# A fused attention and MLP kernel: key sums of batch 0 in a PSUM bank of their own, one load moved, more filler products, and a new order of the whole program

## The chip, the cores and the metric

The kernel runs on one core of a Trainium2 chip. The metric is the time of one execution on the device in microseconds (us). A core has five engines that run side by side, each with its own in-order instruction stream: TensorE (PE in the profile; its weight loads are listed as PEld), VectorE (DVE), ScalarE (ACT), GpSimd (POOL) and SyncE (SP), which here only issues DMA transfers. They meet through semaphores: an instruction that waits holds up everything behind it on its own engine.

## What is computed

The first half is linear attention with a quadratic feature map. With a = x S1^T and b = x S2^T (8 numbers each), the features of a row are the 64 products of a and b. For each of 4 batches and 4 heads, over 1088 rows of 32 numbers:

```python
def phi(x):
    a = np.einsum('rd,bhsd->bhsr', S1, x)
    b = np.einsum('rd,bhsd->bhsr', S2, x)
    return np.einsum('bhsi,bhsj->bhsij', a, b).reshape(*x.shape[:-1], r * r)
q_p, k_p = (phi(q), phi(k))
kv = np.einsum('bhsf,bhsd->bhfd', k_p, v)
z = np.sum(k_p, axis=2)
num = np.einsum('bhsf,bhfd->bhsd', q_p, kv)
den = np.einsum('bhsf,bhf->bhs', q_p, z)[..., None] + 1e-06
return num / den
```

The second half takes the result as 4352 tokens of 128 numbers (x) and applies an MLP with a leaky activation, h = x w_in (128 to 2048), g = max(h, 0) + alpha min(h, 0), out = g w_out. The kernel uses g = (1 - alpha) max(h, 0) + alpha h, so that the MLP is relu(h) times the weights w_a = (1 - alpha) w_out, plus x times one 128x128 matrix W = w_in (alpha w_out).

## The kernel before

Nothing is written in program order. The code makes a list of operations, each with the engines that may run it, an estimated duration, the operations that it depends on, and the buffers that it holds. A list scheduler, `plan()` (L174), walks this list with estimated times, picks an engine and a buffer slot for each operation, and returns the order in which they are emitted. An operation's place is steered by its due time, which is worked out backwards from its users and then moved by a constant from the table `SHIFT` (L65 to L171). The arrival times of the first loads are constants too, in `FIRST` (L371). So a change of constants alone moves hundreds of instructions, and with a place moves the engine and the PSUM bank. On the chip only the emitted order and the semaphores count.

The names of operations, which the text below uses:

- `k0.0T`, `k0.0Tc`, `k0.0ab`, `k0.0abc`, `k0.0kp0` and `kp1`: the keys of batch 0, first half of the row blocks. They are transposed on TensorE (L625), copied to SBUF, multiplied by S1 and S2 (L635), copied to the tile ab (L360 or L362, one helper line for all copies), and multiplied out into the features kp (L652). `k0.1...` is the second half, `kr0.0...` the 64 rows left over. Batches 1 to 3 are transposed on VectorE (L679) and do both halves in one product.
- `kv0.0`, `kv0.1`, `kvr0`: features times v, summed in one PSUM bank (L698, L712), and the sums of the key features, which come from a times b (L704, L715). In the kernel before, both kinds sit in one bank, and the sums are the last products of each of these operations.
- `zm0`, `finz0`, `zc0`: the key sums are spread out (VectorE, L728), multiplied (TensorE, L734), and reduced to the tile zc (VectorE, L740 and L741). `kvc0`, `fin0`, `kvW0` do the same for the sums with v: a copy, a transpose (L743), a copy to the tile kvW.
- `q0.0T`, `q0.0a`, `q0.0b`, `q0.0ac0`, `q0.0ac1`, `q0.0mul0`, `q0.0mul1`: the first 512 queries of batch 0 are transposed (VectorE, L832), multiplied by S1 and S2 in two rounds (TensorE, L849), and multiplied out (a copy, L360 or L362, and a product on VectorE, L861).
- `q0.0den`, `q0.0num` (TensorE, L762), `q0.0dT`, `q0.0rc`, `q0.0rr` (VectorE, L769 to L778: transpose, reciprocal, transpose back), `q0.0x0` (VectorE, L784): the quotient, which is the MLP's input xT. `q0.1...` is the second 512 of batch 0; q1, q2, q3 and qr are the other batches and the left-over rows, with L792, L805 and L819 in place of L832, L849 and L861.
- `h0.0` to `h0.15` (TensorE, L931): 16 products of 128x512 for 512 tokens, four PSUM banks at most in flight; `r0.0` to `r0.15`: relu to bf16 (ScalarE L937, or VectorE L939); `o0.0` to `o0.15` and `W0` (TensorE, L952, or L949 in the last group): products summed in PSUM bank 7. The first number is the group: 0 to 6 have 512 tokens each, 7 to 9 have 256. `oT` and `st` transpose and store.
- `w_in_bf` (cast of w_in, L360), `w_a`, `w_b`, `w_hi`, `w_lo` (made of w_out, L555, L564, L572, and a cast), `winT` (L588), `Wmm` (L597), `W`: the weights are prepared inside the kernel, each in four or two parts, in between the rest.

All loads but three small ones are issued on SP's queue in the order of the code (L445 to L468). The first are k0.0, k0.1, kr0.0, v0.0, q0.0, v0.1, vr0.0, q0.1, w_in0, w_out0, w_in1, w_out1.

Before `h0.0` there is also filler: `dummy()` (L496) multiplies ones into bank 7, whose content is not used. Seven stand at the start (`warm`, L500); `plan()` counts further ones from its own estimate of TensorE's idle time ahead of an operation (L256), and L1013 emits them in front of it:

```python
o.fill = max(0, int((t - free_at["pe"] - 350) / DUMMY)) if 4000 < t < FILL else 0
```

## Time and profile before

| | us |
|---|---|
| median of 5 executions (lowest, highest) | 114.19 (113.84, 115.08) |
| the profiled execution, its own time | 113.85 |
| its span, first to last instruction | 112.1 |
| so outside the span | 1.75 |
| first MLP product `h0.0` starts | 17.30 |
| last product ends, by the chain | 108.84 |

The profile page gives each engine's busy time. The timeline lists runs of like instructions with start and duration; a product's duration there includes its way through the array, so that the distance from one start to the next tells how fast they follow each other. The list of waits says for which engine an idle one waited, and the chain of work that ended last follows, from the last instruction back, what released each step.

### The profile page before, as it was taken

What the parts mean: (1) busy time and instruction counts of PE and PEld (TensorE: products, weight loads), DVE (VectorE), ACT (ScalarE), POOL (GpSimd) and SP (SyncE); (2) the same over time, 40 slices, a digit from 0 to 9 for tenths busy, and PEclk for the clock granted to TensorE, in tenths of its full rate; (3) what the DMA queues carried; (4) which work ended last, traced back from release to release, by engine and by line L of the source; (5) the groups of instructions that cost most, each with busy time, mean ns of one, the idle gap of its engine ahead of it and who ended that gap; (6) DMA issues with size and microseconds to landing.
All of it is one profiled execution on the core that took longest, in us unless ns stands there. A gap on an engine that the chain in (4) does not pass through costs nothing.

```text
span 112.1 us, 3537 instructions
## 1 busy us (share of the span) xinstructions
PE 104.6 (93%) x1455; PEld 54.2 (48%) x1455; DVE 83.3 (74%) x157; ACT 75.5 (67%) x163; POOL 25.3 (23%) x25
## 2 busy tenths in 40 slices
PE   7997777999999999999999999999999999999980
PEld 2664442463664352344466254444334344588970
DVE  3176689896899878989854397748698798788750
ACT  2542589999709863479947474987596197678860
POOL 3060089779800006480000600000000000000000
PEclk9999999999999999999999999999999999999999
DMA  2899899869849961005002200032050022023131
GB/s 77 242 304 280 241 281 314 179 122 340 149 56 327 231 99 29 0 6 94 0 6 47 46 6 0 0 53 46 0 94 0 6 47 47 3 47 61 33 58 47
DMA packets 37536, 11.25 MB, mean 100 GB/s; under 512 B 27008, under 2 KB 37520, under 8 KB 37520
## 3 DMA queue, kind: packets, MB, share of 16 engines
q1 hardware_dynamic: 37264, 10.95, 41.7%
q8 instruction: 11, 0.18, 0.8%
q10 hardware_dynamic: 256, 0.08, 0.3%
q14 instruction: 5, 0.04, 0.1%
HBM read 8.80 MB, written 2.23 MB: 98 GB/s over the span
## 4 chain that ended last, share of the span: by engine, by line
PE 85%; DVE 7%; ACT 3%; issue 1%; POOL 1%; DVEq 0%
PE ps L952 27%; PE ps L931 26%; PE ps L762 8%; PE ps L805 5%; PE ps L635 4%; PE ps L498 3%; PE ps L698 2%; PE ps L849 2%; PE ps L949 2%; PE ps L625 1%; PE ps L734 1%; DVE qT__75 L792 1%; DVE aq__77 L819 1%; DVE aq__76 L861 1%; DVE kT__64 L679 1%
## 5 line engine op out<-in xcount | busy, mean ns | idle before, releaser
L931 PE MATMUL ps<-xT__96,w_in_bf 128*128 128x512 bf16 (+1 forms) x80 | 22.0, 357 | 1.7 <-DVE xT__96 L784 1.3
L931 PEld LDWEIGHTS <-w_in_bf 128*128 128x128 bf16 x160 | 15.2, 97 | 16.7 <-issue 5.0
L952 PEld LDWEIGHTS <-w_a_bf 128*128 128x128 bf16 x144 | 13.5, 98 | 14.3 <-issue 3.2
L931 PE MATMUL ps<-xT__97,w_in_bf 128*128 128x512 bf16 (+1 forms) x80 | 18.5, 337 | 0.0
L937 ACT ACTIVATE rh__82<-ps 128x512 bf16<-128x512 f32 (+1 forms) x21 | 11.5, 548 | 5.6 <-PE ps L931 5.3
L937 ACT ACTIVATE rh__83<-ps 128x512 bf16<-128x512 f32 (+1 forms) x18 | 9.8, 545 | 4.9 <-PE ps L931 4.5
L652 POOL TENSOR_TENSOR kp__70<-ab__67 128x1024 f32<-128x1024 f32 (+1 forms) x3 | 5.0, 1658 | 28.0 <-ACT ab__67 L360 28.0
L937 ACT ACTIVATE rh__85<-ps 128x512 bf16<-128x512 f32 (+1 forms) x19 | 10.8, 566 | 0.5 <-PE ps L931 0.5
L937 ACT ACTIVATE rh__86<-ps 128x512 bf16<-128x512 f32 (+1 forms) x16 | 8.9, 557 | 2.2 <-PE ps L952 1.9
L360 ACT COPY aq__76<-ps 128x1024 f32<-128x1024 f32 (+1 forms) x7 | 5.6, 833 | 5.6 <-PE ps L805 3.5
L937 ACT ACTIVATE rh__84<-ps 128x512 bf16<-128x512 f32 (+1 forms) x15 | 7.8, 519 | 1.0 <-PE ps L931 0.9
L769 DVE STREAM_TRANSPOSE dt__78<-ps 128x1024 f32<-128x1024 f32 (+2 forms) x6 | 5.6, 932 | 3.6 <-PE ps L762 3.6
L952 PE MATMUL ps<-rh__82,w_a_bf 128*128 128x512 bf16 (+1 forms) x22 | 7.8, 354 | 0.0
L952 PE MATMUL ps<-rh__84,w_a_bf 128*128 128x512 bf16 (+1 forms) x21 | 7.6, 360 | 0.0
L952 PE MATMUL ps<-rh__83,w_a_bf 128*128 128x512 bf16 (+1 forms) x20 | 7.3, 364 | 0.0
L937 ACT ACTIVATE rh__87<-ps 128x512 bf16<-128x512 f32 (+1 forms) x12 | 6.8, 569 | 0.6 <-PE ps L931 0.5
L952 PE MATMUL ps<-rh__85,w_a_bf 128*128 128x512 bf16 (+1 forms) x20 | 7.1, 353 | 0.0
L952 PE MATMUL ps<-rh__86,w_a_bf 128*128 128x512 bf16 (+1 forms) x19 | 6.8, 358 | 0.0
L959 DVE STREAM_TRANSPOSE oT__91<-ps 128x512 f32<-128x512 f32 (+1 forms) x8 | 5.4, 681 | 1.3 <-PE ps L952 1.1
L939 DVE TENSOR_SCALAR rh__84<-ps 128x512 bf16<-128x512 f32 x8 | 5.5, 682 | 1.2 <-PE ps L952 1.1
L778 DVE STREAM_TRANSPOSE rr__80<-dt__78 128x1024 f32<-128x1024 f32 (+2 forms) x6 | 5.6, 932 | 0.2
L952 PE MATMUL ps<-rh__87,w_a_bf 128*128 128x512 bf16 (+1 forms) x16 | 5.7, 354 | 0.0
(165 smaller groups left out, 213.8 us busy)
## 6 DMA issues: line engine op xcount, KB each, us to landing
out_dram<-oT__91 SPq DMA_DIRECT2D x28, 64.0 KB, 1.9
k<-in_k_dram SPq DMA_DIRECT2D x3, 512.0 KB, 5.6
q<-in_q_dram SPq DMA_DIRECT2D x3, 512.0 KB
v<-in_v_dram SPq DMA_DIRECT2D x12, 128.0 KB, 6.0
w_in_f<-in_moe_w_in_dram SPq DMA_DIRECT2D x2, 512.0 KB, 8.2
w_out_f<-in_moe_w_out_dram SPq DMA_DIRECT2D x2, 512.0 KB, 6.5
k<-in_k_dram SPq DMA_DIRECT2D x2, 256.0 KB, 2.8
v<-in_v_dram SPq DMA_DIRECT2D x2, 256.0 KB, 3.7
```

Of the source, the lines that this page charges most:

```text
L360: nc.scalar.copy(dst, src)
L635: nc.tensor.matmul(ps(bf)[lo + i:lo + i + aw, j * 64:(j + 1) * 64], sb(bT)[:, j * cnt + i:j * cnt + i + aw], S12blk.rearrange("p h c -> p ...
L652: (nc.vector if e == "dve" else nc.gpsimd).tensor_tensor(out=dst, in0=i0, in1=i1, op=ALU.mult)
L762: nc.tensor.matmul(dst, w, mv, start=True, stop=True, skip_group_check=True)
L769: nc.vector.transpose(bview(sb(dt), [[1, nn]]).rearrange("p (c n) -> p c n", c=2), ps(bd)[:, :, :ncp])
L778: o = op("dve", dv(nn) + 35, lambda e: nc.vector.transpose(sb(rr)[:, :nn], bview(sb(dt)[:, :, 1], [[32, nb], [0, 32]])), [o], [dt, rr], 80 ...
L805: nc.tensor.matmul(ps(bufs[t // 2])[64 * c:64 * c + 64, t % 2, :nf], bview(Sab[32 * t:32 * t + 32, i], [[1, R]]), moving(sb(bq), t, c), st ...
L931: nc.tensor.matmul(ps(b)[:, :n], w_in_bf[:, c * 128:(c + 1) * 128], xs(), start=True, stop=True)
L937: nc.scalar.activation(sb(br)[:, :n], ps(b)[:, :n], ACTF.Relu)
L939: nc.vector.tensor_scalar_max(sb(br)[:, :n], ps(b)[:, :n], 0.0)
L952: nc.tensor.matmul(ps(bo)[:, :n], w, y(), start=c == 0, stop=c == NC)
L959: o = op("dve", dv(n) + 40, lambda e: nc.vector.transpose(bview(sb(boT), [[1, n]]), ps(bo)[:, :n]), [last], [bo, boT], 80, end, f"oT{g}")
```

## The change

There are four parts.

1. For batch 0 the key sums get operations of their own, `z0.0`, `z0.1` and `zr0`, in a bank of their own (`bzs`), which depend on ab alone. `kv0.0`, `kv0.1` and `kvr0` keep the products with v, and `zm0` reads the new bank as soon as `zr0` is done. For batches 1 to 3 the same products stand where they stood.
2. The load of q0.0 is issued one place earlier, before v0.0 rather than after it.
3. Filler is counted with 150 ns rather than 350 ns taken off the planned gap, up to `h0.0` instead of up to a planned 12.5 us.
4. `SHIFT`, `FIRST` and the planned rate of v's later loads have new values, so that the order, the engine and the bank of operations are new in the whole program.

The two programs' opening, in the order in which each engine gets it (a number in brackets: that many fillers ahead; loads left out):

```
TensorE before: warm k0.0T rowsT k0.1T k0.0ab kr0.0T alphaT k0.1ab [2]kv0.0 q0.0a q0.0b kr0.0ab kv0.1
  [1]kvr0 [1]finz0 fin0 q0.0den q0.0num winT0 q0.1a q0.1b h0.0 h0.1 h0.2 h0.3 h0.4 h0.5 h0.6 o0.0 h0.7
  o0.1 o0.2 h0.8 o0.3 k1.0ab q0.1den h0.9 k1.1ab
TensorE after:  warm k0.0T rowsT k0.1T k0.0ab alphaT k0.1ab z0.0 kr0.0T [1]z0.1 kr0.0ab q0.0a q0.0b zr0
  [2]finz0 kv0.0 kv0.1 kvr0 q0.0den fin0 [3]q0.0num [1]q0.1a q0.1b h0.0 h0.1 h0.2 h0.3 h0.4 q0.1den h0.5
  h0.6 h0.7 o0.0 h0.8 o0.1 h0.9 o0.2 o0.3 winT1 h0.10 o0.4 k1.0ab h0.11 h0.12 o0.5 winT0
VectorE before: ... k0.0kp1 q0.0T k0.1kp0 alpha q0.0ac1 q0.0mul0 kr0.0kp q0.0mul1 zm0 q0.1T zc0 q0.0dT q0.0rc
  q0.0rr q0.0x0 q0.1mul0 q0.1mul1 r0.3 k1.0T k1.1T
VectorE after:  ... alpha k0.0kp0 q0.0T k0.1kp0 kr0.0kp q0.0ac1 zm0 q0.0mul1 q0.0mul0 zc0 q0.1T q0.0dT q0.0rc
  q0.0rr w_hi0 q0.0x0 q0.1mul1 q0.1mul0 r0.1 r0.3 q0.1dT r0.4 k1.0T k1.1T
ScalarE before: ... q0.0ac0 kr0.0abc kvc0 w_in_bf kvW0 w_in_bf w_a1 w_hi0 q0.1ac1 q0.1ac0 w_in_bf w_in_bf
  r0.0 r0.2 r0.1 r0.6 r0.7 r0.4 r0.5
ScalarE after:  ... kr0.0Tc kr0.0abc q0.0ac0 kvc0 w_in_bf w_in_bf kvW0 w_b1 w_hi1 q0.1ac1 q0.1ac0 w_in_bf
  w_in_bf r0.2 r0.0 w_b3 r0.7 r0.5 r0.8 r0.6
GpSimd before:  ident identb k0.0kp0 k0.1kp1 w_b0 w_a0 w_lo0 w_b3 w_a2 w_a3 w_b2 w_lo2 k1.1kp k1.0kp
GpSimd after:   ident k0.0kp1 k0.1kp1 identb w_b0 w_a1 w_a0 w_b2 w_lo0 w_lo1 w_a3 w_a2 w_lo3 k1.1kp k1.0kp
```

From `h0.0` on, TensorE's stream of bf16 products is interrupted by the fp32 products of the attention 16 times before and 20 times after. The diff, without the values of `SHIFT`:

```diff
-FILL, DUMMY = 12500, 220.0
+FILL, DUMMY = 20000, 220.0
 AHEAD = {"pe": 120, "act": 150, "dve": 250, "pool": 300, "sp": 0}
...
 SHIFT = {
...
 }
...
     holds = {b.stream: 0 for o in ops for b in o.bufs}
-    mode, count, there = 0, BEFORE, {0: 0.0, 1: 0.0}
+    mode, count, there, begun = 0, BEFORE, {0: 0.0, 1: 0.0}, False
     for o in reversed(ops):
...
         if e == "pe":
-            o.fill = max(0, int((t - free_at["pe"] - 350) / DUMMY)) if 4000 < t < FILL else 0
+            begun = begun or o.name == "h0.0"
+            o.fill = max(0, int((t - free_at["pe"] - 150) / DUMMY)) if 4000 < t < FILL and not begun else 0
             block, count = count // BLOCK, count + 2 * o.fill + o.ni
...
     state = {"t": 0.0}
-    FIRST = {"rows": 3900.0, "arows": 5000.0, "k0.0": 3800.0, "k0.1": 4700.0, "kr0.0": 5250.0, "v0.0": 6350.0,
-             "q0.0": 7350.0, "v0.1": 8300.0, "vr0.0": 8600.0, "q0.1": 9900.0, "w_in0": 11700.0, "w_out0": 13400.0,
-             "w_in1": 15200.0, "w_out1": 17000.0, "k1": 18600.0, "q1": 20400.0}
+    FIRST = {"rows": 4050.0, "arows": 4900.0, "k0.0": 3800.0, "k0.1": 4700.0, "kr0.0": 5900.0, "q0.0": 7100.0,
+             "v0.0": 8150.0, "v0.1": 9000.0, "vr0.0": 9200.0, "q0.1": 9850.0, "w_in0": 11600.0, "w_out0": 13000.0,
+             "w_in1": 15500.0, "w_out1": 17200.0, "k1": 19200.0, "q1": 20900.0}
     loads = {}
...
                  bass.AP(tensor=v.tensor, offset=(b * H * S + 256 * t) * D, ap=[[2 * D, 128], [S * D, H], [1, 2 * D]]),
-                 128 * H * 2 * D * 4, 115.0)
+                 128 * H * 2 * D * 4, 170.0)
 
...
     load_rest("k", k_rs[0], k, 0, (0,), "kr0.0")
+    load_q0(0)
     load_half("v", v_sb, v, 0, 0)
-    load_q0(0)
     load_half("v", v_sb, v, 0, 1)
...
 
-    rest_k = {}
+    rest_k, rest_ab = {}, {}
 
...
         for b in (2 * m, 2 * m + 1) if i is None else (2 * m + i,):
+            rest_ab[b] = o[0].deps[0]
             rest_k[b] = o + got(tag.replace("k", "v", 1))
...
                       lambda bkp=bkp: bview(sb(bkp), [[1, 1024]]), [bab], [bkp], kp_eng[hp], f"k{b}.{hp}", None if pe else turn)
-            halves.append((o, bab, bkp))
+            halves.append((o, bab, bkp, o[0].deps[0]))
         m, i = divmod(b, 2)
         bk = pk()
+        bzs = pk() if pe else bk
+        z0 = 0 if pe else R
+        rest = slice(i * SR, (i + 1) * SR)
+
+        def where(x, h):
+
+            return (x, h) if pe else (h // 2, 2 * x + h % 2)
 
...
             def f(e):
-                ab = [bview(sb(x[1]), [[1, 256]]) for x in halves]
                 kp = [bview(sb(x[2]), [[1, 1024]]) for x in halves]
...
                         for h in range(H):
-                            half, blk = (x, h) if pe else (h // 2, 2 * x + h % 2)
+                            half, blk = where(x, h)
                             nc.tensor.matmul(ps(bk)[32 * h:32 * h + 32, :R], v_sb[b][:, h, 4 * x + t if pe else 2 * t + x],
...
                                              start=x == t == 0, stop=False, skip_group_check=True)
+                if not pe:
+                    zs(xs)(e)
+            return f
+
+        def zs(xs):
+            def f(e):
+                ab = [bview(sb(x[1]), [[1, 256]]) for x in halves]
                 for x in xs:
                     for h in range(H):
-                        half, blk = (x, h) if pe else (h // 2, 2 * x + h % 2)
-                        nc.tensor.matmul(ps(bk)[32 * h:32 * h + 32, R:R + 32], ab[half][:, 32 * blk:32 * blk + 32],
+                        half, blk = where(x, h)
+                        nc.tensor.matmul(ps(bzs)[32 * h:32 * h + 32, z0:z0 + 32], ab[half][:, 32 * blk:32 * blk + 32],
                                          ab[half][:, 128 + 32 * blk:128 + 32 * blk + 32],
-                                         start=False, stop=False, skip_group_check=True)
+                                         start=pe and x == 0, stop=False, skip_group_check=True)
             return f
...
         def kvr(e):
-            s = slice(i * SR, (i + 1) * SR)
             for h in range(H):
-                nc.tensor.matmul(ps(bk)[32 * h:32 * h + 32, :R], v_rs[m][s, h], kp_rest[m][s, h],
+                nc.tensor.matmul(ps(bk)[32 * h:32 * h + 32, :R], v_rs[m][rest, h], kp_rest[m][rest, h],
                                  start=False, stop=True, skip_group_check=True)
+            if not pe:
+                zr(e)
+
+        def zr(e):
             for h in range(H):
-                nc.tensor.matmul(ps(bk)[32 * h:32 * h + r, R:R + r], ab_rest[m][s, 0, h], ab_rest[m][s, 1, h],
+                nc.tensor.matmul(ps(bzs)[32 * h:32 * h + r, z0:z0 + r], ab_rest[m][rest, 0, h], ab_rest[m][rest, 1, h],
                                  start=False, stop=True, skip_group_check=True)
+        oz = None
+        if pe:
+            for x in range(2):
+                oz = op("pe", 150, zs((x,)), [oz, halves[x][3]], [bzs, halves[x][1]], 200, name=f"z{b}.{x}", mode=1, ni=16)
+            oz = op("pe", 140, zr, [oz, rest_ab[b]], [bzs], 200, name=f"zr{b}", mode=1, ni=16)
         o = None
...
             hs = [halves[x] for x in xs] if pe else halves
-            bufs = [bk] + [x for h in hs for x in h[1:]]
-            o = op("pe", 600 * len(xs) + 30, kv(xs), [o] + [x for h in hs for x in h[0]] + (got(f"v{b}.{xs[0]}") if pe else got(f"v{b}")), bufs, 200,
-                   name=f"kv{b}" + (f".{xs[0]}" if pe else ""), mode=1, ni=80 * len(xs))
-        o = op("pe", 260, kvr, [o] + rest_k[b], [bk], 200, name=f"kvr{b}", mode=1, ni=32)
+            bufs = [bk] + [y for x in hs for y in (x[2:3] if pe else x[1:3])]
+            o = op("pe", (500 if pe else 600) * len(xs) + 30, kv(xs), [o] + [x for h in hs for x in h[0]] + (got(f"v{b}.{xs[0]}") if pe else got(f"v{b}")),
+                   bufs, 200, name=f"kv{b}" + (f".{xs[0]}" if pe else ""), mode=1, ni=(64 if pe else 80) * len(xs))
+        o = op("pe", 150 if pe else 260, kvr, [o] + rest_k[b], [bk], 200, name=f"kvr{b}", mode=1, ni=16 if pe else 32)
         bs, bz, bf = Buf("fs"), Buf("fs"), pk()
...
         def zm(e):
-            nc.vector.tensor_mul(bview(zt(), [[32, H], [r, 4], [1, r]]), bview(ps(bk)[:, R:R + 32], [[0, H], [r, 4], [1, r]]),
+            nc.vector.tensor_mul(bview(zt(), [[32, H], [r, 4], [1, r]]), bview(ps(bzs)[:, z0:z0 + 32], [[0, H], [r, 4], [1, r]]),
                                  bview(M16, [[4, H], [1, 4], [0, r]]))
-        o1 = op("dve", dv(128), zm, [o, c_mask2], [bk, bz], 80, due + 31, f"zm{b}")
+        o1 = op("dve", dv(128), zm, [oz if pe else o, c_mask2], [bzs, bz], 80, due + 31, f"zm{b}")
         o2 = op(("act", "dve"), ad(128), lambda e: copy(e, sb(bs), bview(ps(bk), [[0, 2], [1, R]])), [o], [bk, bs], LA,
```

## The prediction

> **What bounds the kernel now.** I read the page first, then TensorE's waits, then the chain of the stretch where they lie, then the timeline around it, and the busy time by stage.
>
> The page, busy share by engine and TensorE's granted clock:
>
> ```profile
> PE 104.6 (93%) x1455; PEld 54.2 (48%) x1455; DVE 83.3 (74%) x157; ACT 75.5 (67%) x163; POOL 25.3 (23%) x25
> PEclk9999999999999999999999999999999999999999
> ```
>
> TensorE's waits, all of them:
>
> ```profile
> PE ps L931 <- DVE xT__96 L784: 1.3, 1, 1.3
> PE ps L498 <- PEq L1028: 0.8, 1, 0.8
> PE ps L712 <- DVE kpr L652: 0.7, 1, 0.7
> PE ps L762 <- DVE zc L741: 0.7, 1, 0.7
> PE ps L931 <- ACT rh__82 L937: 0.2, 1, 0.2
> ```
>
> TensorE waits only in the opening; the largest wait, 1.3, is that of h0.0 for x0. A busy share can deceive, so I looked at the starts. From 18.82 to 108.84 the 512-column products follow each other every 0.216, and what is lost beyond that pace is 0.24 at 33.1 to 33.6, 0.20 at 98.6 and some 0.15 among the last products: 0.6 in 90. The Trainium skill (Perfetto Trace Analysis, Identifying the Most-Contended Engine) says that matmul busy time is no measure of how full TensorE is, and that weight loading is to be taken instead: here 48%, which would make VectorE, at 74%, the engine to relieve and leave TensorE room to catch up. By that rule x0, 0.7 earlier (below), is worth its 0.7. By the row of starts the array's own pace is the limit, and a lead counts only as far as more of TensorE's work is done at a given time. I go by the row. So the change is worth what it does before TensorE fills up, less what it adds to TensorE's stream later.
>
> The chain over 12 to 20 us (start, length, what):
>
> ```profile
> 13.32 1.11 PE ps L762 x32
> 14.43 0.55 PE ps L588 x8
> 14.98 1.16 PE ps L849 x32
> ...
> 16.16 1.07 ACT aq__76 L360 x2
> 17.24 1.03 ACT w_in_bf L360 x2
> 18.27 0.51 ACT rh__82 L937
> ```
>
> The chain does not run through x0. It runs through q0.1a, its two copies, two casts of w_in and the first relu, on ScalarE: h0.4 at 18.82 waits for a bank that r0.0 frees. x0, h0.0 and VectorE are late too, but not the last. The timeline of the engines that feed this (start, length; the bracket is the idle time before):
>
> ```profile
> 12.62 0.62 ACT L360 CAST w_in_bf<-w_in_f 128x512 bf16<-128x512 f32 x1 [0.39 <-DMA w_in_f<-in_moe_w_in_dram]
> 14.22 1.28 ACT L572 ACTIVATE w_a_bf<-w_out_f,omaT 128x128 bf16<-128x128 f32 x4 [0.30 <-DMA w_out_f<-in_moe_w_out_dram]
> 14.34 1.04 POOL L555 TENSOR_TENSOR w_b_f<-w_out_f,alphaT 128x512 f32<-128x512 f32 x1 [5.74 <-DMA w_out_f<-in_moe_w_out_dram]
> 16.55 0.69 DVE L784 TENSOR_TENSOR xT__96<-ps,rr__80 128x512 bf16<-128x512 f32 x1
> ```
>
> w_in0 lands at 12.6 and w_out0 at 14.2. The DMA engines are busy throughout until then (the page shows 8 to 9 tenths), and the change moves no byte of these two loads, so I keep both times.
>
> **The queries' load.** q0.0 now lands about when v0.0 did (6.28 against 7.17), v0.0 about 0.9 later, near 7.2. It gains nothing: q0.0T on VectorE started at 7.19 because k0.0kp1 held VectorE to 7.14, and it does so still. v0.0 is now needed past 10.6. Cover on both sides, so zero; without it, 0.9. On SP's queue nothing else changes place.
>
> **Key sums first.** The number of products is the same; the split adds only places. alphaT moves up 0.2 (kr0.0T leaves), q0.0T runs from 7.15 to 7.87, and q0.0a, no longer behind kv0.0, starts at 7.95 instead of 8.27. Both rounds take 1.12, and in the trace the copies start only when both are done (9.39, then 9.43), so q0.0ac1 starts at 9.15. zr0 is done at 9.45, and VectorE then does ac1 0.61, zm0 0.20, mul1 0.60, mul0 0.60: to 11.2. finz0 is done by 10.7, in their shadow, as are kv0.0, kv0.1 and kvr0 on TensorE (to 11.3). zc0 takes 0.61: 11.8. den starts 0.06 later, 11.87 against 13.32: **1.45 earlier**. From den's start to dT is 0.77, from dT to x0's slot 2.47 (14.09 to 16.55): 15.1.
>
> **But x0 does not run then.** On VectorE it now stands behind w_hi0, the cast of w_b0, which GpSimd makes from w_out0: 14.34 plus 1.04 is 15.38, plus a semaphore and the cast (0.47 by the L362 cast at 28.98; starts follow 0.39 apart) is 15.87. num is no tighter: kvW0 now sits behind two casts of w_in (12.62, then 0.52 each) instead of one, ends at 13.92, and num is through at 14.6. So x0 runs at 15.87 instead of 16.55, and h0.0 at **16.6 instead of 17.30**: half of the 1.45 is swallowed by a load.
>
> **What ScalarE makes of it.** num at 13.98 plus 0.59 and one filler, then q0.1a at 14.87 against 14.91: the chain's own step has not moved. Both rounds 1.12, so the copies start at 16.05 (16.16 before), two copies and two casts take 2.0, and the first relu on ScalarE starts at **18.05 against 18.16**. VectorE, after x0 and two products, has its first relu at 17.95 against 18.64. h0.4 however needs the bank of q0.1mul1, not of a relu: it can go at 17.67 instead of 18.82, which is 1.15.
>
> From that I take what is not done yet: winT0 stands behind h0.4 now, 0.45. And waits: den behind mul0 (0.1 at 17.9), h0.7 behind r0.0 and h0.10 behind r0.7, because ScalarE makes w_b3 (four instructions, 1.19) between r0.0 and r0.7; together 0.19 until h0.10 at 21.15. One more switch into fp32 products: 0.09. 1.15 - 0.45 - 0.19 - 0.09 = **0.42 gained** by then.
>
> **The new order later.** A switch costs what this timeline of TensorE shows:
>
> ```profile
> 25.77 0.38 PE L952 MATMUL ps<-rh__88,w_a_bf 128*128 128x512 bf16 x1
> 25.99 0.38 PE L952 MATMUL ps<-rh__89,w_a_bf 128*128 128x512 bf16 x1
> 26.30 0.27 PE L625 MATMUL ps<-ident,kr 64*128 64x64 f32 x1
> ```
>
> 0.216 from bf16 to bf16, but 0.31 into fp32: 0.093 more, on most of the 16 entries (none where L734 leads, 0.216). Leaving adds nothing beyond the last product's own way. Four more entries, one counted: 3 x 0.093 = **0.28 lost**. Stalls of the new order cannot be read in this trace. I walked it to the second group: kr0.1ab, q0.1num and kv1 each find their copies ready with 0.2 to 0.8 to spare, and r0.14, the last relu of group 0 on ScalarE, ends at 26.6 where TensorE wants it at 27.1. Its bounds: minus 0.6 (all that the old order lost, above) to plus 1.5 (as much as the opening lost between 17.3 and 18.8); I take zero, the same loss as now, since the nearest row is an order of the same planner that loses 0.6 in 90 us.
>
> **Fillers.** Three more (14 against 11), 0.22 each. Two ahead of finz0 and three ahead of num end before zm0 and kvW0 do (9.75 against 10.1, 13.0 against 13.9): zero. The one ahead of q0.1a is on ScalarE's chain and is in the sum (0.1 there). What they might buy is the clock, and it is already granted in full from 4.4 us on, with idle times up to 1.6 in the opening: zero, and not below zero.
>
> Sum against the profiled execution: 113.85 - 0.42 + 0.28 = 113.7. The median of the five is 0.34 above that execution; so **114.0** as a median. 1% (1.1 us) is about what a measurement of this kernel can tell from no change.
>
> **Rivals.**
>
> A, the lead survives. If the relus keep up and the new order loses none of what the old one lost, the gain is 1.15 - 0.45 + 0.6 - 0.1 = 1.2: 113.0. For it: VectorE is free 0.7 earlier, and den 1.45 earlier leaves slack if w_out0 lands sooner in other executions. Against: ScalarE, which ends the chain, is only 0.1 earlier. Chance 0.25.
>
> B, slower: ScalarE starves TensorE in group 0. After r0.4 VectorE has only transposes, ratios and weight parts, so eleven relus in a row (r0.5 to r0.15) and w_b3 fall to ScalarE: 13 relus x 0.49 + 1.19 + 1.1 of other copies = 8.6 from 18.05, 26.6. TensorE's four banks turn over only as fast as these. It decides if ScalarE falls more than 0.5 behind, through a later w_out1 for w_b3 (landed 17.5, wanted at 19.0) or a product late at w_hi3, on which GpSimd's w_lo3 and then k1.1kp wait. Then group 0 slips by w_b3's 1.2 and kv1 by GpSimd's two products (1.9 each): some 1.4 lost, 115.5. For it: the page's ACT row from 14 to 28 us stands at 8 and 9 tenths already. Chance 0.22.
>
> C, the main case, the gain in the opening spent by starving relus and more switches: 114.0, between 113.2 and 114.8. Chance 0.53.
>
> **Numbers.** The range takes in A and B with a margin: 112.7 to 115.6. Faster than 113.05: most of A's lower half and little else, 0.20. Slower than 115.33: B's upper half and unread stalls, 0.23. Within 1%: 0.57.
>
> **What would show it.** Right: den near 11.9, x0 waiting for w_hi0 and starting near 15.9, h0.0 near 16.6, ScalarE's first relu near 18.0, 20 entries at 0.31. Wrong: w_out0 landing well off 14.2 (then x0 moves with it); waits of L931 and L952 for relus between 18 and 28; or, against all of this, gaps in TensorE's stream after 34 us.

## The result, and the profile after

The changed kernel takes 113.53 us (median of 27 runs, 112.63 to 115.94), the kernel before 114.67 in the same comparison (48 runs, 113.79 to 117.65). The ratio is 0.9911, 95% interval 0.9893 to 0.993: about 1.0 us faster, a small change whose interval leaves out no change. The forecast was 114.0, range 112.7 to 115.6. Ratios here compare only executions within 1.5% of the fastest of their kernel, while medians and ranges take all; the profile that was stored first with the changed kernel (own time 115.02) lies outside, so the lines below are from a second one of the same code (run `a_again`, own time 114.24, span 112.5) unless another is named. That one, too, is 0.7 above the median, so what a usual execution is like has to be read from all profiles together, in the table below.

Line numbers have moved: h products are L949 now, o products L970, den and num L780, x0 L802, q0.1's rounds L867 and its products on VectorE L879, copies L356 and L358, relus L955 and L957, filler L494.

The page, engine shares and granted clock:

```profile
PE 104.1 (93%) x1440; PEld 54.3 (48%) x1458; DVE 82.5 (73%) x157; ACT 75.5 (67%) x164; POOL 24.4 (22%) x24
PEclk9999999999999999999999999999999999999999
```

No share has moved by more than two points (some of PE's records are missing, which is why its count is 1440). Nothing of the gain or its cause is to be seen here. TensorE's waits (what waited, for what, total, times, longest):

```profile
PE ps L780 <- issue: 1.2, 1, 1.2
PE ps L494 <- PEq L1046: 0.8, 1, 0.8
PE ps L949 <- DVE aq__76 L879: 0.7, 1, 0.7
PE ps L970 <- issue: 0.6, 4, 0.2
PE ps L752 <- DVE fs__99 L746: 0.4, 1, 0.4
```

The wait of h0.0 for x0 (1.3 before) is gone here (other profiles of the new order list 0.4 to 1.6 for it), and so is den's wait for zc (0.7). In the opening an h product now waits 0.7 for q0.1's product on VectorE. The first row is new and was in nobody's forecast: num stands still for 1.2, and no semaphore explains it ("issue"). The chain over 12 to 20 us:

```profile
13.39 0.65 PE ps L780 x13
14.04 1.15 issue
15.20 0.62 PE ps L780 x3
15.81 0.32 PE ps L494
16.14 1.13 PE ps L867 x32
...
17.30 0.59 ACT aq__76 L356
...
17.91 0.70 DVE aq__76 L879
...
18.66 0.59 PE ps L949 x2
...
19.26 0.67 PE ps L780 x16
```

As before, it runs through q0.1's rounds and not through x0; but it leaves ScalarE after one copy, goes over VectorE's product, and from there to h0.3, h0.4, den of q0.1 and h0.5 (19.96). The casts of w_in and the first relu, which ended it before, are off it. The timeline of what feeds x0:

```profile
12.99 0.27 ACT L356 COPY kvW<-ps 128x128 f32<-128x128 f32 x1
13.38 1.04 POOL L551 TENSOR_TENSOR w_b_f<-w_out_f,alphaT 128x512 f32<-128x512 f32 x1 [4.59 <-DVE dt__78 L787]
14.45 1.25 DVE L358 CAST w_hl<-w_b_f 128x512 bf16<-128x512 f32 x1
15.85 0.69 DVE L802 TENSOR_TENSOR xT__96<-ps,rr__80 128x512 bf16<-128x512 f32 x1 [0.15 <-PE ps L780]
```

w_hi0 does stand in front of x0, and it takes 1.25 there, not 0.47. In this execution x0 then waited for num as well (15.82). In the first stored profile, where w_out0 landed late, at 15.78, the chain is the predicted one, from the load over w_b0 to x0 (the 1.13 of "issue" is w_hi0's time on VectorE):

```profile
6.14 9.64 DMA w_out_f<-in_moe_w_out_dram
15.92 1.05 POOL w_b_f L551
17.03 1.13 issue
18.16 0.69 DVE xT__96 L802
```

**One table for the profiles.** From these traces: where the recorded full clock of TensorE begins, start of q0.0a, start of q0.1a, start of x0, start of the product from which TensorE's stream runs without a further wait of any size (the mark: h0.4 before, h0.5 after), end of the last product. The runs are described in the next section; `b_again`, whose clock was halved behind the mark, is left out.

| execution | full clock | q0.0a | q0.1a | x0 | mark | last | mark to last |
|---|---|---|---|---|---|---|---|
| before | 4.36 | 8.27 | 14.91 | 16.55 | 18.82 | 108.80 | 89.98 |
| before, second profile (`b_again2`) | 9.98 | 10.53 | 17.17 | 18.41 | 21.08 | 111.05 | 89.97 |
| `b_nofill` (old order) | 4.79 | 8.55 | 15.18 | 16.44 | 19.08 | 109.09 | 90.01 |
| after, stored | 6.65 | 8.82 | 16.86 | 18.16 | 20.75 | 110.00 | 89.25 |
| after (`a_again`) | 3.77 | 7.76 | 16.07 | 15.85 | 19.96 | 109.22 | 89.26 |
| `a_zlate` | 6.55 | 8.84 | 16.48 | 17.34 | 20.37 | 109.63 | 89.26 |
| `a_q1early` | 6.11 | 8.68 | 15.58 | 16.09 | 19.98 | 109.24 | 89.26 |
| `a_hi1first` | 13.23 | 10.20 | 17.49 | 17.94 | 21.38 | 110.74 | 89.36 |
| `a_x0first` | 6.01 | 8.68 | 15.35 | 15.52 | 19.24 | 108.76 | 89.52 |
| `a_pad` | 5.08 | 8.14 | 14.52 | 16.51 | 19.04 | 108.25 | 89.21 |
| `a_nofill` | 5.75 | 8.53 | 14.75 | 16.90 | 19.43 | 108.64 | 89.21 |
| `a_oldq0` | 3.42 | 8.44 | 15.26 | 16.89 | 19.42 | 108.63 | 89.21 |
| `a_nofill_w3` | 8.24 | 9.34 | 16.87 | 17.61 | 20.75 | 110.02 | 89.27 |

Three things can be read off. From the mark to the end the time is fixed for each of the two orders, 89.97 to 90.01 before and 89.2 to 89.4 after (`a_x0first` loses 0.26 more, told below): every difference between executions of one order arises in the opening, and after it TensorE only goes at its own pace. The mark itself is, in the new order, q0.1a plus 3.89 or x0 plus 2.53, whichever is later: 16.07 + 3.89 = 19.96, 16.51 + 2.53 = 19.04. `a_q1early` is the exception, by design. And q0.0a, from which the rest of the opening follows, moves with the start of the full clock: 7.76 with the clock from 3.77, 8.53 from 5.75, 8.84 from 6.55, 10.20 from 13.23 (`a_oldq0`, which waits for a load, falls out of this row). In the old order the mark is 10.53 to 10.55 behind q0.0a in all three profiles.

### The profile page after: what moved, and what is told of

Same layout as the page of the kernel before. It is cut to its first block, busy times and chain, and to the rows that moved or that the text cites. A ratio compares the mean times of both kernels' runs of the same rounds, so it can differ in the third digit from the quotient of the medians.

```text
span 113.2 us, 3548 instructions
## 1 busy us (share of the span) xinstructions
PE 107.0 (94%) x1458; PEld 55.2 (49%) x1458; DVE 82.4 (73%) x157; ACT 75.5 (67%) x164; POOL 24.3 (21%) x24
## 4 chain that ended last, share of the span: by engine, by line
PE 78%; DMA 10%; SPq 5%; issue 2%; DVE 1%; POOL 1%; ACT 0%; POOLq 0%
PE ps L949 27%; PE ps L970 27%; DMA w_out_f<-in_moe_w_out_dram 9%; PE ps L780 7%; PE ps L823 6%; SPq L380 4%; PE ps L631 3%; PE ps L701 3%; PE ps L593 2%; DMA out_dram<-oT__91 1%; POOL w_b_f L551 1%; PE ps L584 1%; PE ps L752 1%; PE ps L721 1%; DVE xT__96 L802 1%
## 5 line engine op out<-in xcount | busy, mean ns | idle before, releaser
L949 PEld LDWEIGHTS <-w_in_bf 128*128 128x128 bf16 x160 | 15.2, 97 | 15.7 <-issue 3.9
L949 PE MATMUL ps<-xT__96,w_in_bf 128*128 128x512 bf16 (+1 forms) x80 | 21.4, 358 | 0.9 <-DVE xT__96 L802 0.9
L970 PEld LDWEIGHTS <-w_a_bf 128*128 128x128 bf16 x144 | 13.6, 98 | 13.0 <-issue 1.7
L949 PE MATMUL ps<-xT__97,w_in_bf 128*128 128x512 bf16 (+1 forms) x80 | 19.3, 336 | 0.0
L955 ACT ACTIVATE rh__82<-ps 128x512 bf16<-128x512 f32 (+1 forms) x24 | 13.0, 543 | 4.8 <-PE ps L949 4.4
L955 ACT ACTIVATE rh__83<-ps 128x512 bf16<-128x512 f32 (+1 forms) x21 | 11.9, 568 | 4.0 <-PE ps L949 3.9
L955 ACT ACTIVATE rh__85<-ps 128x512 bf16<-128x512 f32 (+1 forms) x13 | 7.5, 578 | 5.6 <-PE ps L949 3.4
L955 ACT ACTIVATE rh__84<-ps 128x512 bf16<-128x512 f32 (+1 forms) x17 | 9.4, 552 | 0.4 <-PE ps L949 0.4
L648 POOL TENSOR_TENSOR kp__70<-ab__67 128x1024 f32<-128x1024 f32 (+1 forms) x3 | 5.0, 1658 | 20.7 <-ACT ab__67 L356 20.7
L970 PE MATMUL ps<-rh__83,w_a_bf 128*128 128x512 bf16 (+1 forms) x24 | 8.7, 363 | 0.0
L648 POOL TENSOR_TENSOR kp__71<-ab__68 128x1024 f32<-128x1024 f32 (+1 forms) x3 | 5.0, 1659 | 15.1 <-ACT ab__68 L356 8.3
L970 PE MATMUL ps<-rh__82,w_a_bf 128*128 128x512 bf16 (+1 forms) x23 | 8.2, 356 | 0.0
L970 PE MATMUL ps<-rh__84,w_a_bf 128*128 128x512 bf16 (+1 forms) x21 | 7.5, 359 | 0.0
L970 PE MATMUL ps<-rh__85,w_a_bf 128*128 128x512 bf16 (+1 forms) x19 | 6.8, 357 | 0.0
L970 PE MATMUL ps<-rh__86,w_a_bf 128*128 128x512 bf16 (+1 forms) x19 | 6.8, 357 | 0.0
L356 ACT COPY aq__76<-ps 128x512 f32<-128x512 f32 (+2 forms) x7 | 4.5, 651 | 3.3 <-PE ps L823 2.1
L955 ACT ACTIVATE rh__86<-ps 128x512 bf16<-128x512 f32 (+1 forms) x12 | 6.5, 538 | 0.2 <-ACT rh__84 L955 0.2
L955 ACT ACTIVATE rh__87<-ps 128x512 bf16<-128x512 f32 (+1 forms) x12 | 6.5, 541 | 0.0
L957 DVE TENSOR_SCALAR rh__85<-ps 128x512 bf16<-128x512 f32 (+1 forms) x8 | 4.4, 551 | 2.8 <-PE ps L949 2.0
L494 PE MATMUL ps<-const-bfloat16-1.0 128*128 128x512 bf16 x14 | 5.3, 504 | 0.8 <-PEq L1046 0.8
```

What stands on the lines that cost most here:

```text
L356: nc.scalar.copy(dst, src)
L494: nc.tensor.matmul(PS[:, 7], ones(128), ones(512), start=True, stop=True, skip_group_check=True)
L648: (nc.vector if e == "dve" else nc.gpsimd).tensor_tensor(out=dst, in0=i0, in1=i1, op=ALU.mult)
L949: nc.tensor.matmul(ps(b)[:, :n], w_in_bf[:, c * 128:(c + 1) * 128], xs(), start=True, stop=True)
L955: nc.scalar.activation(sb(br)[:, :n], ps(b)[:, :n], ACTF.Relu)
L957: nc.vector.tensor_scalar_max(sb(br)[:, :n], ps(b)[:, :n], 0.0)
```

## The experiments

**The changed kernel once more**, unchanged.

> The changed kernel itself, once more, for a profile that is comparable with that of before. Theory 1 (the lead of the opening): w_out0 lands near 14.2 us, w_hi0 and x0 follow it as in the prediction (x0 near 15.9, h0.0 near 16.6), TensorE reaches the fifth h product near 17.7, and by the first product of group 1 it is 0.4 us ahead of before; ratio 0.99. Theory 2 (the gain is in the stretch after 34 us): h1.0 is no more than 0.1 us ahead, and the gain is found later.

Measured: ratio 0.9929 (0.989 to 0.9968), median 113.64. It agrees with the first comparison; its profile is the one above. That num stood still for 1.15 us here, and q0.1a for 0.7 in other executions, made fillers and order ahead of num the next suspects.

**The kernel before once more**, unchanged.

> The kernel before itself, once more. Its profiled execution of 113.85 us was among the fastest of its executions (median 114.7). Theory 1: a typical execution loses its 0.8 us in the opening, to loads or instructions that come later, and keeps the same pace of 0.216 us per product after 34 us. Theory 2: it loses them as gaps in TensorE's stream after 34 us.

Measured: one execution, 116.91. Busy time by stretch, the column before the last two being the granted clock:

```profile
10.00:13.66 3.66, 1.80 (x43) 1.17 (x51) 2.97 (x8) 1.63 (x5) 0.06 (x1) 1.00 1.00 279
13.66:17.07 3.41, 3.41 (x64) 1.81 (x48) 2.94 (x5) 1.63 (x5) 3.10 (x4) 0.50 1.05 307
17.07:20.49 3.42, 1.57 (x21) 0.62 (x7) 2.18 (x4) 2.93 (x6) 3.42 (x4) 1.00 1.16 296
20.49:23.90 3.41, 3.41 (x9) 0.96 (x7) 3.22 (x6) 2.45 (x5) 0.61 (x1) 0.50 0.64 155
```

The clock was halved twice, for 3.41 us each, in the opening and just behind it. So the sparse opening can lose the clock although the longest wait of TensorE is 1.5 in this profile and 1.3 in that of before (the prediction's 1.6 stands in no list of waits). That the clock is "granted in full from 4.4 us on" held for the profiled execution only.

**No gap filler in the changed kernel**: the seven fillers in gaps are left out, the seven at the start stay. Fillers write nothing that is used.

```diff
     for o in plan(ops, classes):
-        dummy(o.fill)
         o.emit(o.on)
```

> The changed kernel with the order kept and the seven fillers after the start-up ones left out (14 PE instructions fewer). My theory: the fillers buy nothing and the one ahead of q0.1a costs 0.1, so the same or 0.1 us faster than the changed kernel: ratio 0.99 against before. Rival: the fillers keep the granted clock in executions in which the opening has long idle stretches; then without them the clock drops in the opening of some, and the ratio rises to 1.0 or above.

Measured: 0.9869 (0.9826 to 0.9911), median 113.02. q0.1a follows num at once, but it takes 1.82 instead of 1.12: the stand-still has moved into it. With twelve instructions fewer ahead of num it falls six products later (a product is two instructions, its weight load and itself): behind q0.1a's third product, where it was behind num's 13th. One of six executions had a mean clock of 0.985. The interval touches that of the full change, so whether leaving them out gains 0.4 us is not settled.

**No gap filler in the kernel before**, the same edit (four fillers).

> The kernel before without its four gap fillers (8 TensorE instructions fewer ahead of winT0). Theory F: in a typical execution the border of the second block stalls TensorE in winT0, ahead of q0.1a; with eight instructions fewer it falls at the end of winT0, less than 0.1 us later, so 0.0 to 0.2 us faster, ratio 0.998 to 1.0. Theory of the clock: the fillers keep the granted clock; without them it drops in more executions, ratio 1.003 or above.

Measured: 1.0026 (0.998 to 1.0072), but 7 of its 12 executions had a mean clock of 0.97 to 0.985 (115.4 to 117.2 us), against 5 of the 27 of the unedited kernel beside it. So these fillers are not worth zero: with them the loss of the clock was rarer. (This mean counts from the first record of the clock on and doesn't show a late start: the profile of `a_hi1first`, with the full clock from 13.23, has 1.0.) The profile, of 114.16 us and not halved, ends 90.01 after its mark; its full clock begins 0.43 later than in that of before, and q0.0a, h0.4 and the end are 0.26 to 0.29 later. Over all comparisons the unedited kernel before has a mean clock under 0.99 in 11 of 82 executions (0 of 21, 5 of 27, 4 of 23, 2 of 11), the changed kernel in 2 of 36 (2 of 28, 0 of 8).

**Fewer fillers at the start too**: three instead of seven, none in the gaps.

```diff
-    op("pe", 3750, lambda e: dummy(7), due=-1e6, name="warm", ni=14)
+    op("pe", 3750, lambda e: dummy(3), due=-1e6, name="warm", ni=14)
...
-        dummy(o.fill)
```

> The changed kernel without gap fillers and with three start-up fillers instead of seven, 22 TensorE instructions fewer in all. Theory F: the block border moves past the first round of q0.1a, whose stall of 0.7 us shrinks to below 0.3, and the kernel is another 0.3 to 0.5 us faster, ratio 0.983. Theory G: no change against the kernel without gap fillers, 0.987. A third possibility: the clock is granted later with fewer start-up products and the opening is slower, 0.99 or above.

Measured: 1.0022 (0.997 to 1.0073), median 116.25 (113.6 to 117.78). In the profile the recorded full clock begins at 8.24 and is lost again:

```profile
8.20:11.60 3.40, 2.38 (x66) 1.36 (x62) 2.72 (x7) 1.38 (x4) 1.75 (x3) 1.00 1.09 285
11.60:15.10 3.50, 3.50 (x90) 2.45 (x90) 2.18 (x5) 0.56 (x2) 1.87 (x2) 0.51 1.06 284
```

The four fillers at the start that it lacks, against the run without gap fillers, are worth 1.5% by the ratios (1.0022 and 0.9869) and 3.2 us by the medians of all executions (116.25 and 113.02).

**Same number of instructions, less filler time**: no gap fillers, and at the start five whole fillers and nine of 64 columns. That makes 14 fillers ahead of num, one more than the 13 of the changed kernel, so that TensorE's 512th instruction, at num's 13th product there, lies one product earlier here. (512 is the 450 instructions that the stored profile, whose records are complete, has up to the stand-still, and the 62 that the program's constant `BEFORE` counts ahead of them.)

```diff
-    op("pe", 3750, lambda e: dummy(7), due=-1e6, name="warm", ni=14)
+    op("pe", 3750, lambda e: (dummy(5), small(9)), due=-1e6, name="warm", ni=14)
...
-        dummy(o.fill)
...
+    def small(n):
+        for _ in range(n):
+            nc.tensor.matmul(PS[:, 7, :64], ones(128), ones(64), start=True, stop=True, skip_group_check=True)
```

> The changed kernel without its seven gap fillers, but with two of the seven start-up fillers replaced by nine of 64 columns: the same number of TensorE instructions ahead of num as in the changed kernel, but no filler in any gap. Theory F (instruction blocks): TensorE stands still in num because its 512th instruction is not yet fetched; the same count brings the same stall back, num stands 0.5 to 1.2 us, and the ratio is that of the changed kernel, 0.992. Theory G (occupancy): the fillers themselves cost time by standing in front of real products; without them the time is that of the kernel without gap fillers, 0.987.

Measured: 0.9906 (0.9863 to 0.9948), median 113.54: the same as the changed kernel, but the interval also holds the 0.987 of the other theory, so the time tells neither from the other. No stand-still in its profile, although the 512th instruction lies within one product of where it did, and so x0, not q0.1a, sets the mark (16.51 + 2.53). What differs is when TensorE's next block of instructions came. In `a_again` one packet of 16,384 bytes on the instruction queue went from 12.60 to 13.73, and num went on at 15.20, 1.47 after its end; here it went from 11.31 to 12.41, and num's 12th product, at 14.16, came 1.75 after its end. The packet of `a_again` in the DMA view of 12.5 to 13.8 us:

```profile
q1 hardware_dynamic: 631, 0.32, 97.5%
q8 instruction: 1, 0.02, 5.4%
```

It shares the DMA engines with the loads (q1), but that does not make it slow: it takes 1.13 here, and 1.10 in `a_pad`, where the loads took 68.9%. What differs is when it begins. Of the ten profiles of the new order, four show a stand-still, of 0.5 to 1.2; in them the packet ended at 13.5 to 14.7, and TensorE went on 1.3 to 1.5 after that. In the other six (`a_x0first`, `a_oldq0`, `a_pad` and `a_zlate`, where it ended by 12.7, and `a_hi1first` and `a_nofill_w3`, where TensorE itself was late) TensorE came to that place 1.7 or more after the packet's end. What makes the packet early or late was not tried; since kernels with and without edits are on both sides, it looks like a matter of the execution.

**x0 first**: w_hi0 behind q0.1's two products on VectorE, not ahead of x0.

```diff
-    for o in plan(ops, classes):
+    order = plan(ops, classes)
+    at = {o.name: i for i, o in enumerate(order)}
+    hi = order.pop(at["w_hi0"])
+    order.insert(at["q0.1mul0"], hi)
+    for o in order:
```

> The changed kernel with the cast w_hi0 moved on VectorE from ahead of q0.0x0 to behind q0.1mul0; nothing else moves. My theory: x0 no longer waits for w_out0, h0.0 starts up to 1.3 us earlier (near 15.4), but the relus are where they were on ScalarE, so the end moves by less than 0.2 us. Rival: x0 bounds the kernel; the end moves by 0.7 us or more, ratio 0.983.

Measured: 0.9927 (0.9896 to 0.9958), median 113.66: no gain. x0 starts at 15.52 and h0.0 at 16.40, but the mark stays with q0.1a (15.35 + 3.89 = 19.24), and w_hi0 now delays r0.1: h0.6 and a later product come 0.26 later together. So w_hi0 in front of x0 is a real cost (x0 starts 6.84 after q0.0a here, 8.37 in `a_pad`), and taking it away is worth nothing where q0.1a comes next.

**The old place of the queries' load**: v0.0 ahead of q0.0 again.

```diff
-    load_q0(0)
     load_half("v", v_sb, v, 0, 0)
+    load_q0(0)
```

> The changed kernel with q0.0 and v0.0 loaded in the old order, everything else as it is. My theory: the move of this load is worth nothing, since q0.0's transpose waits for VectorE until after its landing; ratio within 0.2% of the changed kernel's. Rival: q0.0 lands 0.9 later, the transpose waits for it, and den and all behind it move by up to 0.5 us.

Measured: 0.9921 (0.9889 to 0.9954), median 113.60. q0.0 lands at 7.65 instead of 6.0 to 6.8, and the time is that of the change: the move of the load is worth nothing that six executions can show. The reason, that VectorE holds the transpose back anyway, does not hold in this profile. The chain of its opening begins with the load:

```profile
3.19 4.46 DMA q<-in_q_dram
7.65 0.02 issue
7.68 0.72 DVE qT__74 L850
8.40 0.04 issue
8.44 1.12 PE ps L867 x32
```

VectorE waited 0.50 for the load, and TensorE 0.58 for the transpose, a wait that no other profile of the new order lists. Its full clock began at 3.42; `a_again`, with 3.77, started q0.0a at 7.76. Where the clock comes at 6 or later, q0.0a starts at 8.68 or later with the early load too, and 8.44 would be in time.

**Key sums late again** in the changed order, in a bank that is free then. Here and below, `behind(x, y)` takes operation x out of the order and puts it right behind y.

```diff
+    next(b for b in at["z0.0"].bufs if b.cls == "ps").slot = 4
+    for x, y in (("z0.0", "kvr0"), ("z0.1", "z0.0"), ("zr0", "z0.1"), ("q0.0mul0", "q0.0mul1"), ("zm0", "zr0"),
+                 ("finz0", "zm0"), ("zc0", "finz0"), ("q0.1T", "zc0"), ("q0.0den", "q0.1T")):
+        behind(x, y)
```

> The changed kernel with the key sums of batch 0 late again: z0.0, z0.1 and zr0 stand behind kvr0 on TensorE (in a bank that is free then), and zm0, finz0 and zc0 follow both of q0.0's products, as in the kernel before; all else is unchanged. If x0 is set by w_hi0 and w_out0's landing (step 4 of the prediction), den may start some 0.7 to 1.0 later and x0 hardly moves; what moves is num, and with it q0.1a, which stands behind den: 0.3 to 0.5 later, so the end is 0.3 to 0.5 later, a ratio to before near 0.995 where the changed kernel has 0.991 to 0.993. If the early key sums are worth what den gains (rival), the end moves by 0.7 to 1.4: ratio 0.998 to 1.004. If they are worth nothing because TensorE stands still at its 512th instruction anyway: 0.991 to 0.993.

Measured: 0.999 (0.997 to 1.001), median 114.25. That is 0.8% above the change: undoing the key sums alone gives back nearly all of its gain. The chain of its opening:

```profile
13.81 0.67 PE ps L780 x16
14.47 0.26 PE ps L761
14.73 0.65 PE ps L494 x3
...
15.43 0.80 PE ps L780 x16
...
16.48 1.20 PE ps L867 x32
```

den starts 4.97 after q0.0a (8.84), against 4.01 in `a_again` (7.76 to 11.77): 0.96 later. In this order den, fin0 (L761), kvW0, num and q0.1a follow one another, so num (6.59 after q0.0a, 5.63 in `a_again`) moves by the same 0.96, and q0.1a with it (7.64 after q0.0a, 6.67 in `a_x0first`, which had no stand-still either). The first theory, 0.3 to 0.5, was too low; the rival, that the lead counts nearly in full, holds within this order. With fin0 ahead of den, as in the kernel before, late key sums might cost less; that was not run.

**All three waits ahead of the relus taken apart**: kvW0 between the casts of w_in, no filler ahead of q0.1a, w_hi1 behind q0.1's copies on ScalarE, w_hi0 behind q0.1's products.

```diff
+    at["q0.1a"].fill = 0
+    cast = [o for o in order if o.name == "w_in_bf"][1]
+    order.remove(cast)
+    order.insert(order.index(at["kvW0"]) + 1, cast)
+    behind("w_hi1", "q0.1ac0")
+    behind("w_hi0", "q0.1mul0")
```

> The changed kernel with the three waits ahead of the relus taken apart at once: kvW0 between the two casts of w_in, not behind both; no filler ahead of q0.1a; w_hi1 behind the copies of q0.1 on ScalarE; w_hi0 behind q0.1's two products on VectorE, so that x0 and these go first. If the end is set by the later of q0.1's rounds and x0 (last product 92.0 after the one's end or 91.7 after the other's start), both are 0.6 to 0.9 earlier and so is the end: ratio 0.983 to 0.987. If TensorE's stand-still at its 512th instruction takes the place of kvW0 as what num waits for, q0.1a stays at 15.3 to 16.0 and the ratio is that of the changed kernel, 0.991 to 0.993. If w_hi1 and w_hi0, moved behind, delay the first relus by as much as they were ahead, no gain either.

Measured: 0.9955 (0.9922 to 0.9988), median 113.81: by the ratios 0.4% above the change (0.9911), with intervals that just overlap. q0.1a came at 15.58 (num stood still for 0.6 here too), but the chain went another way:

```profile
17.28 0.59 ACT aq__76 L356
17.88 0.52 ACT w_hl L356
18.39 1.04 ACT w_in_bf L356 x2
19.43 0.51 ACT rh__82 L955
...
19.98 0.86 PE ps L949 x3
```

w_hi1 sits behind the copies now, and copies, w_hi1, two casts and a relu end later than VectorE's product and den do: from q0.1a to h0.5 it is 4.40, not 3.89.

**The same with w_hi1 left where it was.**

```diff
-    behind("w_hi1", "q0.1ac0")
```

> As the last kernel (kvW0 between the casts of w_in, no filler ahead of q0.1a, w_hi0 behind q0.1's products), but with w_hi1 left ahead of q0.1's two copies on ScalarE, as in the changed kernel. That kernel's traces gave one sum: in every one whose bound was ScalarE the last product ended 89.9 after ScalarE's first relu. If that relu ends the chain of the opening, w_hi1 (0.62) ahead of the copies lies in the time in which ScalarE waits for q0.1's rounds anyway, the first relu comes 0.4 to 0.6 earlier than with w_hi1 behind them (15.4 after q0.1's first product is read from that trace as 3.74; here 3.1 to 3.3), and the ratio goes from 0.9955 to about 0.990. If TensorE's own pace or q0.1's rounds alone decide, the place of w_hi1 is worth nothing and the ratio stays at 0.993 to 0.998.

Measured: 0.9908 (0.9873 to 0.9943), median 113.61. (In the text on record "15.4 after" is a slip; 3.74 is the distance from q0.1a to the first relu.) That distance is 3.22 here (17.49 to 20.71), q0.1a to h0.5 is 3.89 again, and the ratio is 0.5% lower, as foretold; the two intervals overlap. So ScalarE's path and VectorE's run nearly level in this opening: 0.5 us more on ScalarE makes it the later one. Taking away the other waits, on the other hand, gained nothing against the change.

**The kernel before, one more profile.**

> The kernel before, unchanged: one more profile, because the profiled execution of the prediction (113.85) was among its fastest and its usual time is some 0.7 above that. If instruction blocks that arrive late explain the usual time, TensorE stands still at its 512th instruction, or q0.0num is late, and ScalarE's first relu comes 0.5 to 1.0 after 18.16; the time is 114.4 to 115.0. If it is the clock, the granted clock drops to half for 3.4 us somewhere and the time is above 115.3.

Measured: 116.12. No stand-still and no half clock later on, but the full clock came late. The first key transposes:

```profile
3.99 1.08 PE L625 MATMUL ps<-ident,k 128*128 128x128 f32 x4
5.00 0.28 PE L515 MATMUL ps<-ident,rows 16*128 16x16 f32 x1
5.22 1.11 PE L625 MATMUL ps<-ident,k 128*128 128x128 f32 x4
```

The second four took 1.11 where the profiled execution of before took 0.66, and it stays so until 9.98, where the recorded full clock begins (4.36 there). q0.0a starts at 10.53 instead of 8.27. From h0.4 on the two executions agree to 0.01 (89.97 and 89.98).

## Why the prediction was right and where it was wrong

The direction of its main case, a small gain in the opening, was right; the size was not. Its sum was a gain of 0.14 (0.42 won, 0.28 lost), and 1.0 came. That 113.53 is so near to 114.0 is in part luck: 114.19, from which 114.0 was reckoned, was a median of five, and 0.14 less than the 114.67 of 48 executions is 114.5. Step by step:

- **TensorE's own pace after the opening**: right, and more exactly than claimed. Nine profiles of the new order, with marks from 19.04 to 21.38, end 89.2 to 89.4 later (and one, with waits that the edit made, 89.52). The rule weighed there (the Trainium skill, Perfetto Trace Analysis, Identifying the Most-Contended Engine), by which weight loads at 48% leave TensorE room to catch up, does not hold here: no lateness of the opening was caught up in any of them. (Beside weight loads the section names the share of the peak rate, MFU, which the prediction left out and nobody worked out here.)
- **The queries' load**: zero is what the times show (`a_oldq0`). Its cover was thinner than it was said to be: in the trace of before VectorE was free at 7.14 and the load landed at 7.17, and in `a_oldq0` the load came last by 0.50 and was on the chain.
- **Key sums 1.45 earlier**: 1.04 by the distance from q0.0a (13.32 - 8.27 = 5.05 before, 4.01 after). The other part, q0.0a 0.32 earlier, hides behind the clock, with which q0.0a moves from 7.76 to 10.20. Between `a_again` (clock from 3.77, q0.0a at 7.76) and `a_nofill` (5.75, 8.53), a clock from 4.36 as in before would give about 8.0, an estimate: 0.3 earlier than 8.27, as foretold. That "half of the 1.45 is swallowed by a load" is how the stored profile went. In `a_again` x0 started at 15.85, and 15.87 was foretold, but this is luck: w_hi0 began at 14.45 already, took 1.25, and num, which had stood still, came last. But the step missed what the lead pays for: the new order puts fin0 behind den, and num behind two casts of w_in. Without early key sums that order alone puts q0.1a 0.96 later (`a_zlate`). q0.1a "has not moved" against the kernel before is the sum of these two.
- **x0 behind w_hi0**: right in mechanism. The term for the cast was mis-sized, 1.25 for 0.47; GpSimd was at work beside it then. It is in the chain of the stored profile, and x0 sets the mark in `a_pad`, `a_nofill` and `a_oldq0`; elsewhere q0.1a does.
- **h0.4 no longer behind a relu**: right. The prediction had it 0.38 ahead of ScalarE's first relu (18.05 - 17.67); in `a_again` it is 0.43 (19.30 - 18.87), and before it was 0.66 behind. Its price for winT0 behind h0.4, 0.45, is also what the trace has (8 products, 0.056 apart).
- **The step that failed is the cost put on the new order**: 0.19 for waits, 0.09 and 0.28 for four more entries into fp32 products, less nothing for what ends. Measured from mark to end, the new order is 89.98 - 89.26 = 0.72 shorter. Before, den of q0.1 stood in the full stream:

```profile
21.44 0.66 PE L762 MATMUL ps<-aq__76,zc 64*32 64x256 f32 x16
22.03 0.39 PE L931 MATMUL ps<-xT__96,w_in_bf 128*128 128x512 bf16 x1
```

Now it stands ahead of the mark (19.26 in the chain of `a_again`), where h0.5 could not have gone before 19.9 in any case: r0.2 on ScalarE, the relu for which it waits in `a_q1early`, ends at 19.91. Of the 0.72, 0.22 is h0.4, which lies ahead of the mark now, and 0.59 is den; winT0 goes the other way, 0.45; and 0.24 is the wait at 33.1, which the new order does not have. That makes 0.60; entries into fp32 products are 0.10 more. Those cost nothing extra: there are 20 against 16, but five of the 20 start at the plain pace (0.216) or sooner, against two of the 16. Beyond 0.216 the 20 cost 1.43 in sum (in the stored profile, whose records are complete) and the 16 1.41; 0.12 of the 1.43 is den's own entry, ahead of the mark, so behind it 1.31 stands against 1.41. The exception was in the prediction's own text, for L734 (one of its three entries, at 40.32, costs 0.37 all the same); it was not counted on the new order, where L752 and L761 lead four times so, and once a product follows those of Wmm. In `a_again`:

```profile
65.79 0.38 PE L970 MATMUL ps<-rh__85,w_a_bf 128*128 128x512 bf16 x1
66.01 0.27 PE L761 MATMUL ps<-ident,fs__100 128*128 128x128 f32 x1
```

- **Fillers at zero, and never below**: the second half was wrong. Those in front of num and q0.1a cost little or nothing that could be measured (0.9869 without them, 0.9911 with them, intervals that touch); without those of the kernel before, half-clock stretches were more frequent (7 of 12 against 5 of 27).
- **The rivals**: B, ScalarE starving group 0, did not come: the stored profile lists four waits of TensorE in all, none for a relu, and the mark to the end is constant. A, the lead survives, foresaw 113.0: the measured gain lies between A and the main case, and in part by A's reason, since the new order does lose less than the old one.
- **What stays open**: the 0.72 is not the gain, since at the new mark more of the work is done, and it comes later. Counted from q0.0a, the last product ends 100.5 later in all three profiles of the old order and 100.1 to 100.2 later in `a_pad`, `a_nofill`, `a_oldq0` and `a_x0first`. So 0.4 is shown where nothing stands still. In the two profiles of the unedited changed kernel, which both stand still, it is 101.2 and 101.5, more than before: neither shows the gain. The 0.3 ahead of q0.0a is an estimate, and the remaining 0.3 of the 1.0 has no owner, because nobody knows how often executions without a profile stand still or get the clock late. No run gives the old order the early key sums, so what these are worth there is open too.

## What to carry to other kernels

Where one engine is full after the opening, find the instruction from which its stream has no wait, and compare two orders by two numbers: how early that mark is, and what is left to do from it. Work that a change moves from the full part into a wait ahead of the mark (here den and h0.4, 0.8 us) counts, less what the mark itself moves by it; a chain made shorter ahead of the mark counts only until the next of several nearly equal chains takes over. Before two profiles of an opening are compared, see where the full clock begins in each, and count from the first product behind it that both have. Undo a part inside the new order before calling it worthless: the early key sums left q0.1a where it was in the kernel before, yet without them the new order loses almost all that it gains.

## What was not expected of the hardware

- In four of the ten profiles of the new order TensorE stood still for 0.5 to 1.2 us behind its 512th instruction, until 1.3 to 1.5 after the end of a 16,384-byte packet on the instruction queue (13.73 to 15.20 in `a_again`). The profile calls this "issue".
- The full clock begins at very different times in executions of one program (4.36 and 9.98 for the kernel before, 3.77 and 6.65 for the changed one), and with it q0.0a (10.53 - 8.27) and h0.4 (21.08 - 18.82) are each 2.26 later in the first pair. The Trainium skill (TensorE: Matmul & The Clock Gate, Part 1: The HAM clock gate) says that the number of slow products at the start varies from run to run, which these traces show, and puts the cost below 1% of a usual kernel's span; here the two executions differ by 2%.
- The clock was halved in windows of 3.41 us in an opening whose longest wait is 1.5 (`b_again`). The same page (HAM oscillation) warns of gaps above about 3.4; shorter ones were enough here. TensorE was busy for 1.80 of the 3.66 us ahead of the first such window and for 1.57 of the 3.42 ahead of the second. That is no threshold: `a_nofill_w3` lost the clock after 2.38 of 3.40, and `a_pad`, busy for half of the 3.41 from 15.32 on, kept it.
- VectorE's cast of 128x512 from fp32 to bf16 took 0.38 to 0.42 in `a_zlate`, `a_q1early` and `a_hi1first`, where GpSimd was idle for most of it, and 1.25 in `a_again`, `a_pad` and the stored profile, where GpSimd was in its products throughout. TENSOR_SCALAR of 128x16 took 0.18 in the stored profile, where GpSimd was idle, and 0.76 in `a_zlate`, during a product. The cast of `a_zlate`:

```profile
17.03 0.38 DVE L358 CAST w_hl<-w_b_f 128x512 bf16<-128x512 f32 x1
17.26 1.06 POOL L551 TENSOR_TENSOR w_b_f<-w_out_f,alphaT 128x512 f32<-128x512 f32 x1 [1.23 <-DMA w_out_f<-in_moe_w_out_dram]
```
